# Turning probability tiles by a DMA round over DRAM and VectorE blocks instead of TensorE

## The chip, the cores and the metric

The kernel runs on one core of a Trainium2 chip. The metric is the device time in microseconds of one execution. The core has five engines with queues of their own, worked off in order: TensorE (PE; its weight loads are PEld), VectorE (DVE), ScalarE (ACT), GpSimd (POOL) and SyncE (SP, which here only issues DMAs). All DMAs of this kernel go through SP's queue and run on the core's 16 DMA engines.

## The reference

Two stages in float32. First an attention for 8 batches x 8 heads, 576 tokens, 64 values a head, whose scores below the row's maximum minus `tau` are dropped:

```
scores = q @ k.T / 8;  keep scores >= rowmax(scores) - tau
attn = exp(kept - rowmax) / (sum + 1e-9);  x = attn @ v
```

Then, for each batch, a gated layer over the 576 x 512 matrix x of all heads: `h = gelu(x @ w_in)` is split into u and v, v is normalized over its 512 columns and mixed over the tokens by `w_sg` (576 x 576, plus a bias), and the output is `x + (u * mixed v) @ w_out`.

## The kernel before, in words

Two heads are handled together as a pair; there are 32 pairs (n = 0 to 31), four of each batch. The 576 tokens are 4 row tiles of 128 and a tail of 64. A pair has 9 tiles (h, i): four whole row tiles of each head, and one (i = NM = 4) that holds the tails of both heads. For each tile:

- TensorE computes the scores of 128 rows against 576 keys into PSUM (L835; L810 and L824 in the first four pairs). From pair 4 on q and k are split into a high and a low fp32r part, which needs three products.
- VectorE takes the negated row maximum (L844), GpSimd makes the threshold of it (L850), ScalarE the exponentials (L871), written to a tile p in SBUF that holds 576 columns of each head, and VectorE zeroes what lies below the threshold and sums the rows (`select`, L878). There are two p tiles, used in turn.
- For the product with v the keys must lie on the partitions, so p is transposed. For each tile four 128x128 blocks go through TensorE into one PSUM bank (`transposes`) and ScalarE copies the bank to SBUF as the turned tile pt (`place`, L1001). The keys beyond 512 are turned and copied apart (`tail_transposes`, L1016).

In 27 pairs (n = 4 to 30; `by_rows` is true there, and `moved` with it) the whole row tiles of head 1 don't go to TensorE straight from p: `move` (L887) first copies their 512 columns by a DMA from SBUF to SBUF into a tile m of type fp32r, and TensorE turns m (L541, `turn_moved`). There are two rooms for m, used in turn. Tiles of head 0 and the tail tiles are turned as float32 (L538, `turn`).

P x V (`values`, L1027) then runs for 256 and for 320 columns of rows, both heads in two halves of the same bank. The row sums are inverted, sent to DRAM (L947) and fetched back spread over the partitions (L952 to L954); VectorE multiplies them in (L1036); the result x is kept as a high and a low part (L1047, L1052).

The gated layer of a batch (products at L1126) runs when the four pairs of its batch are done, in pieces between the scores of the next batch's pairs. The last batch's layer stands alone at the end.

All work is cut into steps, collected in `plan`. A table of 5476 places (`PLACES`) says in which order the steps are issued; each engine works off its own instructions in that order. Besides this, a planner in the kernel's build goes through the steps in that order with assumed durations and picks for each PSUM tile one of the 8 banks (`bank_of`).

Of the kernel before, what the change touches and what calls it, by code (L numbers as in the profile page):

```python
# [22 lines left out]
P = 128  # L23
# [11 lines left out]
PLACES = (  # L35
    "c-qZa3v^ZGmA>D9&b{ZJ`@YG2<^7NlNFWd1fdGO6Di&)Mb+lAkbzC#*npxAaUB#tst=h*b>ddqbOO{%7Xlt!)t!<}8+X@A-JmewBoA3q`z+iY9"
    "k~81_Pog|RAP^jna?id0+5f-y{`R*YCmzS~c-;Rx|H;k0cYf>q>TymHX#Yf@y-V5lQ+Ay4`N<y7NqbIRJxSO(d8w;yZSvDOb=${}Pdnwzr(Hkr"
    "oT|y`g|j_foZa5t?laH!^zdx-^4XqK?RF1z;G8aY#{O;=&h9{mp3}(Jjh=27y4BNmN(%JE{B!x^oZ*jidOGy79;XvG=ThkLoK4U9;^tg151dOI"
    "pC0++oR2@wNy5&>;&y5M=|w$V1n{&1;`AU-oll(yXX^2s<JgnCsB@NuGqSM@+`6LIxfS;yf1Dop(_=kd^36GCU+4xm=REm#0bxI@9?z$qKWE10"
    "Q>+KhS!jGlh@Fe$!8y$LT!cSe^=;>T)1@c=c+P@bw~6cYoClth>ZsFQy7YwC=fKVBQG7fX;?D()g*}=>x}V>ii>{;2X>;$HRr36QJKbRBUi&?#"  # L40
    "_ss6Eb3H#z!0ATBxxiDLi!tx4BA3*0ryIw6$5p4Ni=V3F=MT!IK=Cu`xaR_~Isc>E|Nk6!dg@2-z|g&h&t#5YiuixFbKG-*aqI=hdlHs&g4jFm"
    "IK7cmM!Tb4yD?!Oi<!z%cjIf<1&#(ni9VZ$s<Fzkec);W2mYbWOu=U#n_^7A_1fQmTV<jj-f0{d@_tS~3X~ywXmXpm3(0*+Zz?loYspZU@#c6="
    "!?aP;zJl2|KAJ!ArrKEYo7bSYZtB~0bp{YnkquA%=5YgA$VTGM2cNwoo`}FM#gfUp`-4|9g8Os(HI$k_Fp;{ad}O?Y+maYFX?R-{@FNPtGwwik"
    "IRyf@#~K0=e0ank2Q05DTmxSasV4ga8z$nhjj-VlBl}&OdMhJu!W%8ZAuJ8SXO6<c0yKgW3I9d}QH(bH7KobJ8Q_48GI@ks3bsFYgjNMhtaqrd"
    "IJgnVxNPRcRs%+v8MNNxG6vx9{OpU}sRcX&gR!gv%{0mM;R9F^1ta{E5Hc!}!fnq7fgJu<_T$3L(L)rs(%1~sAH%`$hkO>SP|K*>NEz7br@u&U"
    "rzLTozsly9zSxk9BL*#wU^hRLF!1XdlmiOp+CrjANz~T(9v8bqM$UR3S!{lQCcz|(1N=;Sfx~>L^05wf$jZ&e^9C$jjyG?>Vhf6R?xAcEPncz)"
# [12 lines left out]
    "K>f6Bj}92yy4ouegLK_dsE*p0CDrU!{PZsRA#m5@FG{Ddft8TzI9Rp98~JY09O}ufx&K+>c4Z^KTRA#U4N@jxycZ`HA@PEWi>dYm{3pEiq2D2N"
    "IE2!ef%$g4xugI)Yw$Bau|!{ciDLW<a18sDl&h@VR(pK<xp7rIyC(YGS;TEH)6#48!5UL)MSsF2#OQEP;Yzd^Y=FovzzS~4LNy!YD=^zr<!G$J"  # L60
    "JXozhvl@%oqKIl5>y0c*4+*xQ(p)f%bIZ0w;kW;j{!H8>S(q?a>oQYGxJctHe`3@tx++wwMzvoEaf@^v){Viw&CDMa=9!Ik_?8c*rLOi7KRZ|$"
    "-HRhia6`U<{_52)<Y3a=e?G8cD)rPc%_C+av{|Cgx^qzaCae-RYFQadA|8|JAlKzPCb6OG?#X^ytDBUUC19!e6Dr=z9N;M#<hA2AJbc9sgrGR@"
    "=?7SM?)ekH`-b8z4O0O_vP%|*VWIFHWyXGnjhm}UCFS^yDlYy=@o@6s4*W$2u?kBJ@-B<vU2RBykF__I)nMks!nfSoRgynb#iUT4kV=S;_jQ8e"
    "YV~J*#9;bmFmU$mn5CzTn@FjZibmgzmq-%wEvN=zo-lAMq1deo#NJ`YnU*UakRi3A_@V!1|C#i@w8S$1aw&N<s72~d7AJ!SJuvh`&{)H7u?ct?"
    "e(tV8%wp8z!2;|U$NW*D5c}L)f?Gc2-TF3=Ghqc5<ui{kEpNtiu0Mn+OLr0z{pgp_OI?n|U=?7%4vT|9vj$696b*F)`M6Yh{Y<r`eFa?GixHR)"
    "<)cl<Da%3~&H?M&jnixXixX5Zu<Cm9dVnE%3e_f^mILWV3%n=1QAU)hQCz6@U>ggccRJb3`1qs{%@v6+W6nhUjcX(tIZsH(GUrxme@3MCG9$K^"
    "3vMIxANis5(`K4!XV4%Bv#RXK+e$in>&<zZ2j#kab0MkuX0vG~@Umk55;x5^*0)M5=Y-34cbH(LC{QRd%AWmFP)2~k@77B_&~3ViF3VMmZA$7("
    "s8rXTC{f<V?!{D!&_VhW8O;3R;3#wX)~o0v!d`N5iPX6ab7}>W(rEg$BtyfVt|~Fx%&%l_f0cS({+eWat{$UulO|8w&o&*Hh>f~^mopqIq`p;Z"
    "Y!ny1fZ6gTiKe^s#MqHP25%AeP<biIv5wd(_~c7N>lfCqDBd}Y7FV#$7(N3>rM`KYeKIdda>y-%u}Zh=JUxuC0c7Fp^5v_T`F;GELzS5;z$!x5"
    "hDSIiYgBZ?%k{dRf&%(`iUsSdQY-?tz{&MAXQo_}wI&SRLZf&<3tCaRWlML+5;w~Ae%j#WAi(*`X74lQ!B0iX<g~B3<<;WQ{l}7S5SF=9B<Wd="  # L70
# [12 lines left out]
)
LAST_SCALE, SIGMA, SPREAD = 0.55, 1.155, 0.7
# [5 lines left out]
ROOMS = 2  # L90

# [5 lines left out]

ENGINES = ("tensor", "vector", "scalar", "gpsimd", "sync")

DELAY = dict(  # L100
    tensor=dict(tensor=0, vector=196, scalar=197, gpsimd=224, sync=190),
    vector=dict(tensor=230, vector=127, scalar=128, gpsimd=155, sync=120),
    scalar=dict(tensor=260, vector=146, scalar=153, gpsimd=170, sync=135),
    gpsimd=dict(tensor=205, vector=68, scalar=68, gpsimd=100, sync=67),
    sync=dict(tensor=1180, vector=907, scalar=978, gpsimd=983, sync=900),
)
BEGIN = 575.0
DMA_ISSUE, DMA_ISSUE_PART, DMA_START, DMA_LANES, DMA_BYTES = 525, 690, 650, 8, 250.0

WINDOW, WINDOW_BUSY, CLOCK, STREAM, PER_MATMUL = 10240 / 3, 3200 * P, 2.4, 2.333, 9.7  # L110

RESHAPE = 165


def time_of(engine, op, out, args, sums=False):

    n = out.size // out.shape[0]
    pointers = sum(a.size == a.shape[0] for a in args) if n > 1 else 0
    args = args or [out]
    half = out.shape[0] < P and n < 512  # L120
    if op == "memset":
        return n / 1.2 + (175 if engine == "gpsimd" and half else 35)
    if engine == "tensor":
        if op == "transpose":
            return n * (1 if args[0].dtype == F32R else 2) / CLOCK + (8 if args[0].dtype == F32R else 2.3)
        if args[0].dtype == F32:
            return n * 4 / CLOCK * (0.5 if min(out.shape[0], args[0].shape[0]) < P else 1.0) + 4
        return n / STREAM + PER_MATMUL
    if engine == "scalar":
        return n / 1.2 + (51 if args[0].psum else 93) + 93 * pointers + 115 * half  # L130
    if engine == "vector":
# [3 lines left out]
        elif op == "bn_stats":  # L135
            n = args[0].size // args[0].shape[0]
# [1279 lines left out]
```

## Time and profile before

| | |
|---|---|
| median of 3 runs | 961.41 us (961.38 to 962.68) |
| span of the profiled execution | 959.4 us |
| instructions | 20206 |
| DMA share of the 16 engines, dynamic queue | 45.6% |
| moved by DMA | 128.74 MB, mean 134 GB/s |
| HBM read, written | 46.40 MB, 9.56 MB |

The span runs from the first to the last instruction of the profiled execution; the time of that execution itself isn't recorded apart, and the median of the runs lies 2.0 us above its span. Busy time of an engine is the union of its instructions' durations. Matmuls overlap, so the mean duration of one is longer than its step in the chain. The clock of TensorE is granted in full (1.00) from 24 us on.

### The profile page before, as it was taken

The page shows a single profiled execution, that of the slowest core. Times are in us where ns is not written, and L with a number is a line of the kernel's source. Part 1 is how long each engine was busy: PE and PEld are TensorE (multiplying, and loading weights), DVE is VectorE, ACT ScalarE, POOL GpSimd, SP SyncE. Part 2 cuts the span into 40 slices and gives each one's busy share as a digit, 9 for nine tenths or more (in the row PEclk, how much of TensorE's full clock was granted, in tenths as well). Part 3 has the DMA queues.
Part 4 walks back from the last instruction along what each step waited for, and adds up shares of the span by engine and source line. Part 5 has one row for each costly group of instructions (what it writes and reads, how often), then busy time and mean ns, then how long its engine had stood idle before and what let it go on. Part 6 is the DMA issues. An engine that isn't in the chain of part 4 may idle for free.

```text
span 959.4 us, 20206 instructions
## 1 busy us (share of the span) xinstructions
PE 936.8 (98%) x6822; PEld 800.2 (83%) x6822; DVE 663.8 (69%) x1407; ACT 667.1 (70%) x1395; POOL 564.4 (59%) x997
## 2 busy tenths in 40 slices
PE   7999999999999999999999999999999999999998
PEld 4555889987798888998888898888889888898898
DVE  7899975767777567666786568766677757765451
ACT  5987886767875677665777677766787567764552
POOL 5865665555644577446763557536675366644467
PEclk9999999999999999999999999999999999999999
DMA  8353145465545553555445554456535455341001
GB/s 299 111 143 99 61 123 148 149 185 158 149 129 151 158 147 118 136 162 167 136 133 158 153 153 141 133 142 185 156 119 153 141 160 155 98 127 52 20 7 50
DMA packets 75791, 128.74 MB, mean 134 GB/s; under 512 B 16948, under 2 KB 25383, under 8 KB 75688
## 3 DMA queue, kind: packets, MB, share of 16 engines
q1 hardware_dynamic: 75688, 127.45, 45.6%
q8 instruction: 54, 0.88, 0.4%
q14 instruction: 49, 0.40, 0.1%
HBM read 46.40 MB, written 9.56 MB: 58 GB/s over the span
## 4 chain that ended last, share of the span: by engine, by line
PE 77%; ACT 7%; DVE 7%; DMA 3%; POOL 3%; issue 2%; SPq 0%; POOLq 0%; DVEq 0%; ACTq 0%
PE all_banks L1126 36%; PE all_banks L1027 14%; PE all_banks L835 14%; PE all_banks L538 8%; PE all_banks L541 3%; ACT p L871 2%; DVE nm L844 2%; DVE p L878 1%; DMA m<-p 1%; ACT pt L1001 1%; POOL ot L1331 1%; DMA qz<-qhi 1%; PE all_banks L810 1%; DVE gt L1112 1%; ACT vv L1218 1%
## 5 line engine op out<-in xcount | busy, mean ns | idle before, releaser
L871 ACT ACTIVATE p<-all_banks,nm 128x576 f32<-128x576 f32 x256 | 184.6, 742 | 92.5 <-DVE nm L844 90.6
L844 DVE TENSOR_REDUCE nm<-all_banks 128x1 f32<-128x576 f32 x288 | 208.7, 751 | 52.5 <-PE all_banks L835 43.3
L878 DVE SCALAR_TENSOR_TENSOR p<-all_banks,nm,p 128x576 f32<-128x576 f32 x256 | 204.2, 813 | 48.3 <-POOL nm L850 27.2
L1001 ACT ACTIVATE pt<-all_banks 128x512 f32<-128x512 f32 (+1 forms) x320 | 163.9, 554 | 19.4 <-PE all_banks L538 11.4
L835 PE MATMUL all_banks<-ks,qst 128*128 128x288 f32 x560 | 157.1, 314 | 1.4 <-ACT pt L1001 0.6
L850 POOL TENSOR_TENSOR nm<-columns,nm 128x1 f32<-128x1 f32 x288 | 55.0, 195 | 147.6 <-DVE nm L844 134.5
L1027 PE MATMUL all_banks<-pt,rv 128*64 128x256 f32 (+1 forms) x1024 | 137.8, 411 | 0.0
L835 PE MATMUL all_banks<-kl,qz 128*128 128x288 f32 x448 | 123.6, 295 | 0.0
L538 PE MATMUL all_banks<-ident_r,p 128*128 128x128 f32 x720 | 115.7, 276 | 3.1 <-DVE p L878 2.3
L835 PEld LDWEIGHTS all_banks<-ks,qst 128*128 128x128 f32 x560 | 102.1, 188 | 14.6 <-issue 6.9
L1126 PE MATMUL all_banks<-wsh,z 128*128 128x288 f32 (+2 forms) x512 | 113.4, 298 | 0.3 <-DVE uu L1109 0.3
L1027 PEld LDWEIGHTS all_banks<-pt,rv 128*64 128x64 f32 x1024 | 69.5, 136 | 48.6 <-issue 6.1
L538 PEld LDWEIGHTS all_banks<-ident_r,p 128*128 128x128 f32 x720 | 84.9, 141 | 20.0 <-issue 6.5
L1126 PEld LDWEIGHTS all_banks<-wsh,z 128*128 128x128 f32 x512 | 85.1, 188 | 2.4 <-issue 1.4
L835 PEld LDWEIGHTS all_banks<-kl,qz 128*128 128x128 f32 x448 | 84.5, 189 | 0.2
L1126 PE MATMUL all_banks<-xh,wih 128*128 128x288 f32 (+2 forms) x256 | 77.0, 301 | 0.2 <-ACT ot L1328 0.2
L1126 PE MATMUL all_banks<-gh,woh 128*128 128x288 f32 (+2 forms) x256 | 76.6, 300 | 0.0
L1126 PE MATMUL all_banks<-xl,wih 128*128 128x288 f32 (+2 forms) x256 | 76.0, 297 | 0.0
L1126 PE MATMUL all_banks<-xh,wil 128*128 128x288 f32 (+2 forms) x256 | 75.8, 296 | 0.0
L1126 PE MATMUL all_banks<-gh,wol 128*128 128x288 f32 (+2 forms) x256 | 75.8, 297 | 0.0
L1126 PE MATMUL all_banks<-wsl,z 128*128 128x288 f32 (+2 forms) x256 | 75.7, 297 | 0.0
L1126 PE MATMUL all_banks<-gl,woh 128*128 128x288 f32 (+1 forms) x240 | 70.7, 296 | 0.0
(147 smaller groups left out, 2202.2 us busy)
## 6 DMA issues: line engine op xcount, KB each, us to landing
m<-p SPq DMA_DIRECT2D x108, 256.0 KB
rk<-in_kT SPq DMA_DIRECT2D x32, 320.0 KB
rv<-in_vP SPq DMA_DIRECT2D x32, 320.0 KB
ks<-khi SPq DMA_DIRECT2D x56, 160.0 KB
rq<-in_qT SPq DMA_DIRECT2D x31, 288.0 KB
qz<-qhi SPq DMA_DIRECT2D x56, 144.0 KB
qst<-qhi SPq DMA_DIRECT2D x56, 144.0 KB
qst<-rq SPq DMA_DIRECT2D x56, 144.0 KB
```

The lines of the kernel that those rows point to most:

```text
L538: nc.tensor.transpose(out, x, ident_r.bitcast(F32))
L541: nc.tensor.transpose(out.bitcast(F32R), x, ident_r)
L810: nc.tensor.matmul(st["s", h, i][:, a, 0:HALF], st["q"][rows, qo:qo + P], st["k"][rows, lo:lo + HALF], start=True, stop=True)
L835: nc.tensor.matmul(sc[:, a, 0:HALF], w, x, start=(j == 0), stop=(j == len(terms) - 1))
L844: nc.vector.tensor_reduce(nmax, st["s", h, i][:, :, 0:HALF], AX.XY, ALU.max, negate=True)
L850: nc.gpsimd.tensor_tensor(thr, toff, st["nm", h, i], ALU.subtract)
L871: nc.scalar.activation(target(h, i), st["s", h, i][:, :, 0:HALF], AF.Exp, bias=st["nm", h, i])
L878: nc.vector.scalar_tensor_tensor(dst, st["s", h, i][:, :, 0:HALF], st["thr", h, i], dst, ALU.is_ge, ALU.mult, accum_out=st["l"][:, c:c + 1])
L1001: nc.scalar.activation(dst, src, AF.Copy)
L1027: nc.tensor.matmul(acc[h * D:(h + 1) * D, 0:w], st["v"][:, o:o + D], unit(h, a)[:, kt, 0:w] if kt < NM else tail_unit(a)[:, 0:w], start=(k ...
L1112: put("stt1", end, lambda: nc.vector.scalar_tensor_tensor(t["tmp"], t["tmp"], GELU_C, t["acc"], ALU.add, ALU.mult))
L1126: nc.tensor.matmul(st["acc"], *term(j), start=(j == 0), stop=(j == n - 1))
```

## The change

In the 27 pairs the whole row tiles of both heads are turned without TensorE. The constant `TURNED = (0, 1)` names the heads; `Q = 32` is the block's edge.

- `put_blocks` copies the 512 columns of a tile by one DMA into a DRAM tile d of the shape (4, 128, 128): column group, row, column. Each row of p goes out in four pieces of 512 bytes. There are four d tiles, used in turn.
- `get_blocks` reads d back by one DMA into a tile m (still two rooms): partition 32 g + j gets the rows 4 j to 4 j + 3 of column group g, 2 KB in one piece.
- `turn_blocks` is one VectorE transpose of 128x512 in 32x32 blocks, from m to the turned tile pt. Within a block it reads columns that lie four floats apart, and writes rows that lie four floats apart.

After this, partition p of block k of the turned tile holds key 4 p + k, where before it held key 128 k + p. So `layout` sends v's rows of those pairs in that order, and the tail tile of these pairs, which TensorE still turns, is read with a step of four columns. For the turned tiles no PSUM bank is filled and `place` is not called.

The order of issue is another one (5584 steps, table `ORDER`), and the PSUM banks come from a table too (`FIRST_BANKS`); the planner is gone from the build. In the new order a pair's last turns and its product with v stand among the scores of the next pair, and between the put and the get of a tile stand other DMAs of the same queue.

```diff
+TURNED = (0, 1)
+Q = 32
...
-        moved = by_rows
+        turned = TURNED if by_rows else ()
...
-        def move(h, i):
+        def put_blocks(h, i):
+
+            def f():
+                st["d", h, i] = dram.tile([P // Q, P, P], F32, tag="d", name=f"d{n}_{h}_{i}", bufs=4)
+                nc.sync.dma_start(st["d", h, i].rearrange("g q c -> q g c"),
+                                  st["p", i][:, h * KW:h * KW + MAIN].rearrange("p (g c) -> p g c", g=P // Q))
+            return f
+
+        def get_blocks(h, i):
             tag = slot("m", ROOMS)
 
             def f():
-                st["m", h, i] = ppool.tile([P, MAIN], F32R, tag=tag, name=f"m{n}_{h}_{i}")
-                nc.sync.dma_start(st["m", h, i].bitcast(F32), st["p", i][:, h * KW:h * KW + MAIN])
+                st["m", h, i] = ppool.tile([P, MAIN], F32, tag=tag, name=f"m{n}_{h}_{i}")
+                nc.sync.dma_start(st["m", h, i], st["d", h, i].rearrange("g (j a) c -> (g j) (a c)", a=P // Q))
+            return f
+
+        def turn_blocks(h, i):
+
+            def f():
+                a, j = divmod(i, 2)
+                nc.vector.transpose(unit(h, a)[:, :, j * P:(j + 1) * P].rearrange("p c (j a) -> p a c j", j=Q),
+                                    st["m", h, i].rearrange("p (a k c) -> p a c k", a=P // Q, k=Q))
             return f
...
-                    if moved and i < NM and h:
-                        turn_moved(out, st["m", h, i][:, kt * P:(kt + 1) * P])
-                    else:
-                        turn(out, pt[:, o + kt * P:o + (kt + 1) * P])
+                    x = pt[:, o:o + MAIN]
+                    turn(out, x.rearrange("p (k c) -> p c k", c=NM)[:, kt] if turned else x[:, kt * P:(kt + 1) * P])
...
-            if moved and i < NM and h:
-                at("move", g, move(h, i))
-            at("t", g, transposes(h, i))
-            at("hi", g, place(h, i))
+            if i < NM and h in turned:
+                at("move", g, put_blocks(h, i))
+                at("fetch", g, get_blocks(h, i))
+                at("turn32", g, turn_blocks(h, i))
+            else:
+                at("t", g, transposes(h, i))
+                at("hi", g, place(h, i))
...
+    strided = vv[:, :, :, :main].reshape(b, h // 2, 2, P, main // P, d).transpose(0, 1, 3, 4, 2, 5)
+    for n in range(WHOLE_SCORES, b * h // 2 - 1):
+        vm[divmod(n, h // 2)] = strided[divmod(n, h // 2)]
```

## Rows read from the trace of the kernel before

**Rows 1.** The page, busy us of each engine, share of the span, instructions.
```profile
PE 936.8 (98%) x6822; PEld 800.2 (83%) x6822; DVE 663.8 (69%) x1407; ACT 667.1 (70%) x1395; POOL 564.4 (59%) x997
```
**Rows 2.** Windows: stretch, length, busy PE, PEld, DVE, ACT, POOL, clock, DMA share, GB/s.
```profile
105.00:865.00 760.00, 751.90 (x5613) 659.68 (x5611) 530.90 (x1114) 538.51 (x1117) 444.69 (x781) 1.00 0.51 145
...
40.00:80.00 40.00, 37.25 (x235) 22.31 (x233) 38.69 (x87) 34.64 (x78) 27.38 (x51) 1.00 0.43 122
80.00:120.00 40.00, 39.02 (x258) 29.14 (x255) 37.91 (x87) 33.00 (x73) 22.69 (x53) 1.00 0.26 79
```
**Rows 3.** The chain of waits from 105 to 865 us, shares by line.
```profile
by line: PE all_banks L1126 40.6%; PE all_banks L835 16.6%; PE all_banks L1027 16.2%; PE all_banks L538 9.1%; PE all_banks L541 3.9%; DMA m<-p 1.7%; ACT pt L1001 1.1%; DMA qz<-qhi 1.1%; issue 1.0%; ACT p L871 1.0%; DVE nm L844 0.9%; DVE gt 
```
**Rows 4.** Pieces of the chain: start us, us, what.
```profile
504.00 0.30 PE all_banks L541 x4
...
527.24 0.44 PE all_banks L538 x4
```
**Rows 5.** Timeline of weight loads: start us, us, line, operation.
```profile
526.94 0.49 PEld L538 LDWEIGHTS all_banks<-ident_r,p 128*128 128x128 f32 x4
527.40 0.42 PEld L541 LDWEIGHTS all_banks<-ident_r,m 128*128 128x128 f32 x4
527.77 0.19 PEld L1126 LDWEIGHTS all_banks<-wsl,z 128*128 128x128 f32 x1
```
**Rows 6.** Groups by line from 105 to 865 us: busy us, mean ns, idle before.
```profile
L1001 ACT ACTIVATE pt<-all_banks 128x512 f32<-128x512 f32 x216 | 123.5, 594 | 14.4 <-PE all_banks L538 7.0 <-PE all_banks L541 6.6
```
**Rows 7.** Waits over the span: who for whom, us in total, times, longest.
```profile
ACT p L871 <- DVE nm L844: 90.6, 104, 3.2
DVE nm L844 <- PE all_banks L835: 43.3, 57, 4.7
```
**Rows 8.** Groups by line and form on VectorE, whole span.
```profile
L844 DVE TENSOR_REDUCE nm<-all_banks 128x1 f32<-128x576 f32 x288 | 208.7, 751 | 52.5 <-PE all_banks L835 43.3 <-ACT tt L1016 2.9 <-PE all_banks L810 1.4
...
L1199 DVE BATCH_NORM_STATS2 bn<-vv 128x6 f32<-128x512 f32 x32 | 22.1, 690 | 0.9
L1109 DVE SCALAR_TENSOR_TENSOR vv<-gt,all_banks 128x512 f32<-128x512 f32 x32 | 21.9, 683 | 11.0 <-ACT gt L1114 10.2 <-POOL z L1234 0.5
...
L1036 DVE TENSOR_TENSOR ir<-all_banks,ir 128x320 f32<-128x320 f32 x32 | 15.6, 486 | 5.6 <-PE all_banks L1027 4.7 <-DMA ir<-ld 0.7
L1036 DVE TENSOR_TENSOR ir<-all_banks,ir 128x256 f32<-128x256 f32 x32 | 13.3, 416 | 10.9 <-PE all_banks L1027 4.9 <-DMA out_T<-ot 4.5 <-DMA ir<-ld 1.3
...
L606 DVE TENSOR_SCALAR w<-room 128x512 uint32<-128x512 uint32 x8 | 5.8, 733 | 0.2
...
L598 DVE TENSOR_SCALAR all_banks<-room 128x512 uint32<-128x512 uint32 x8 | 5.5, 684 | 0.1
```
**Rows 9.** Timeline of VectorE, three reductions in a row.
```profile
533.59 2.10 DVE L844 TENSOR_REDUCE nm<-all_banks 128x1 f32<-128x576 f32 x3
```
**Rows 10.** DMA issues: out<-in, engine, count, KB each.
```profile
m<-p SPq DMA_DIRECT2D x108, 256.0 KB
```
**Rows 11.** Windows of the first loads, columns as in rows 2.
```profile
2.00:6.00 4.00, 3.18 (x8) 2.10 (x7) 1.75 (x5) 0.66 (x2) 0.69 (x2) 1.00 0.90 267
6.00:10.00 4.00, 2.49 (x9) 1.19 (x10) 3.45 (x11) 1.25 (x3) 2.40 (x3) 0.78 1.02 399
```
**Rows 12.** SP's issue times of single lines: ns min/median/max, first and last start.
```profile
L1334 SPq DMA_DIRECT2D out_T<-ot x64: 332/398/1101, 153.5 to 956.7; - x64
...
L730 SPq DMA_DIRECT2D rv<-in_vP x32: 328/432/768, 7.4 to 868.8; - x32
```
**Rows 13.** Waits of SP's queue, over the span.
```profile
SPq L887 <- DVE p L878: 143.3, 72, 17.0
SPq L1334 <- POOL ot L1331: 74.5, 18, 29.9
```
**Rows 14.** Timeline of SP's issues: row sums to DRAM, then back.
```profile
543.23 0.30 SPq L947 DMA_DIRECT2D ld<-ir  x1
546.00 0.47 SPq L952 DMA_DIRECT2D ir<-ld  x1
```

More of the change, by code (lines that the diff above doesn't have):

```diff
@@ L3 @@
 from collections import namedtuple
-from contextlib import ExitStack, contextmanager
+from contextlib import ExitStack
 from functools import partial
@@ new lines @@
+FIRST_BANKS = (
+    "c-k$JNdmwi2m=8D|NrA=VlQ13vOz>t_iXgk=`FpRk2qP8+ci;}t)h&*dhOjhvDK&4rkZnC$C0%iqrwNJPF=a}>{SQY>Qv!YhK_YW0Ti#h%nO6y>ST|P("
+    "_LjP`inF?QUrL#d25HZxvD?y??gtZKxQOFM@P^Bc3c6hO9eRfM5oYHJ*dW4mnl?sxxSB9uxMG61WlU);z!!Sg231MY7`Bu$%7;*)P-2)kfC6u3*TvPhe"
+    "XAnMLft)vJQr_nuV3AB1ls?-EchPe1b$;t)pxG-@#@}vWgIR0SpEvlbJ77R4FTD$mg*J$h)2<4@AexhY-`xf8Ki?3ofh}9HM(^od@uyUU+miav}{5&=)"
+    "VAH#%kxy$mmVp-Fi=4!M!L>g2ASg)-q%dWPxhtu-?`3!M<v8{S&^KlNd<DD^t4WuRJbk5~EDli>jyQNnVG6Pv70V=$K`Wp6Iz?mEm}={?oh=0px(gn2&"
+    "A847F"
@@ L107 @@
[L107 to L131, printed above, removed]
-        fast = op == "tensor_scalar" and not args[0].psum
-        if op == "tensor_reduce":
-            n = args[0].size // args[0].shape[0]
-        elif op == "bn_stats":
-            n = args[0].size // args[0].shape[0]
-        return n / (1.92 if fast else 0.96) + 69 + (60 if pointers else 0) + (60 if sums else 0)
-    if engine == "gpsimd":
-        if n == 1 and op == "tensor_tensor":
-            return 464 if pointers else 150
-        if len(out.shape) == 4:
-            return 149 + n + 140
-        return 149 + n * (1.0 if op == "tensor_scalar" else 2.103) + (115 if half or 1 < n < 8 else 0)
-    if out.tile.dram:
-        return out.size * 0.44
-    return out.size * (4 if n >= P else 8) / DMA_BYTES
@@ L149 @@
-class View:
-    def __init__(self, tile_, places, dtype):
-        self.tile, self.places, self.dtype = tile_, places, dtype
-        self.shape, self.size, self.psum = places.shape, places.size, tile_.psum
-    def __getitem__(self, key):
-        return View(self.tile, self.places[key], self.dtype)
-    def bitcast(self, dtype):
-        return View(self.tile, self.places, dtype)
-    def broadcast_to(self, shape):
-        return View(self.tile, np.broadcast_to(self.places, shape), self.dtype)
-    def rearrange(self, pattern, **sizes):
-        left, right = ([g.strip("()").split() for g in _groups(side)] for side in pattern.split("->"))
-        for group, total in zip(left, self.shape):
-            known = 1
-            for name in group:
-                known *= sizes.get(name, 1)
-            for name in group:
-                sizes.setdefault(name, total // known)
-        names = [name for group in left for name in group]
-        x = self.places.reshape([sizes[name] for name in names])
-        x = x.transpose([names.index(name) for group in right for name in group])
-        return View(self.tile, x.reshape([int(np.prod([sizes[n] for n in g])) for g in right]), self.dtype)
-    def area(self):
-        w = self.tile.width
-        first = self.places if self.tile.dram else self.places[0]
-        bits = np.zeros(w, np.uint8)
-        bits[first.ravel() % w] = 1
-        lo, hi = (int(self.places.flat[i]) // w for i in (0, -1))
-        return min(lo, hi), max(lo, hi) + 1, int.from_bytes(np.packbits(bits).tobytes(), "big")
@@ L487, in bank @@
         k = bank_of(name)
-        return psum.tile([P, 512], F32, tag=k, name=name) if k == BANKED else all_banks[:, k[0], :]
+        return psum.tile([P, 512], F32, tag=k, name=name) if k == BANKED else all_banks[:, k, :]
     def two_banks(name):
         k = bank_of(name)
-        return psum.tile([P, 2, 512], F32, tag=k, name=name) if k == BANKED else all_banks[:, k[0]:k[0] + 2, :]
+        return psum.tile([P, 2, 512], F32, tag=k, name=name) if k == BANKED else all_banks[:, k:k + 2, :]
     ident_r = cpool.tile([P, P], F32R, name="ident_r")
@@ L538, in turn @@
         nc.tensor.transpose(out, x, ident_r.bitcast(F32))
-    def turn_moved(out, x):
-        nc.tensor.transpose(out.bitcast(F32R), x, ident_r)
     def warm_up():
@@ L983, in f @@
                     out = tp[:, kt * P:(kt + 1) * P]
-                    if moved and i < NM and h:
-                        turn_moved(out, st["m", h, i][:, kt * P:(kt + 1) * P])
-                    else:
-                        turn(out, pt[:, o + kt * P:o + (kt + 1) * P])
+                    x = pt[:, o:o + MAIN]
+                    turn(out, x.rearrange("p (k c) -> p c k", c=NM)[:, kt] if turned else x[:, kt * P:(kt + 1) * P])
             return f
@@ L1360, in tile_threshold_attention_gated_mlp, with table @@
     issue(plan)
+def table():
+    data = np.frombuffer(zlib.decompress(base64.b85decode(ORDER)), np.uint8).astype(np.uint16).reshape(2, -1)
+    order = np.cumsum((data[0] * 256 + data[1]).astype(np.int16).astype(int)).tolist()
+    banks = list(zlib.decompress(base64.b85decode(FIRST_BANKS)))
+    assert sorted(order) == list(range(len(order)))
+    return order, banks
 _INS = ["qT", "kT", "vP", "w_in", "g_ln", "w_sgT", "b_sg", "w_out"]
@@ L1402 @@
     args.append(nc.dram_tensor("out_T", (b, h * d, s), F32, kind="ExternalOutput").ap())
-    planner = Planner()
-    tile_threshold_attention_gated_mlp(planner, *args, planner.rehearse, lambda name: BANKED)
-    order = planner.order()
+    order, banks = table()
+    banks = iter(banks)
     def issue(plan):
@@ L1412 @@
     with tile.TileContext(nc) as tc:
-        tile_threshold_attention_gated_mlp(tc, *args, issue, planner.bank_of.get)
+        tile_threshold_attention_gated_mlp(tc, *args, issue, lambda name: next(banks))
     r = run_bass_kernel_spmd(nc, [arrays], core_ids=[0])
```

338 lines of the change are left out of this document (82 added, 256 removed).

## The prediction

> **What bounds the kernel now.** I read the page's busy lines first, then the windows, then the chain of waits over the stretch that the change touches. The busy lines show TensorE at 98% of the span and every other engine at 70% or less [rows 1]. The windows say where: from 105 us, just before the first moved tile, to 865 us, just after the last, TensorE works 751.9 of 760 us at full clock, VectorE 530.9, ScalarE 538.5, and the DMA engines are busy half of the time [rows 2]. The chain over this stretch is made of TensorE pieces: the two transposing lines hold 9.1% (L538) and 3.9% (L541) of it, while no line of another engine has 2% [rows 3]. So here TensorE is the bound, and an instruction taken from it is worth its full time until something else is late. The change lies wholly in this stretch (27 pairs; pairs 0 to 3, pair 31, the weights and the last batch's end keep their work), so I leave the other 199.4 us of the span (959.4) as they are. The median of the runs, 961.4, is 2.0 us over the span; I add that at the end.
>
> **What it removes.** 27 pairs x 4 row tiles x 2 heads = 216 groups of four transposes: 108 of head 1 (L541, from the moved tile) and 108 of head 0 (L538, straight from p). On the chain four of L541 stand for 0.30 us and four of L538 for 0.44 us [rows 4]; by the starts of the weight loads, which hold the hand-over too, the four take 0.37 and 0.46 us [rows 5]. So 108 x (0.30 + 0.44) = 80 us, at most 108 x (0.37 + 0.46) = 90 us. I take 80: TensorE's work in the stretch falls from 751.9 to 672 us. ScalarE loses the 216 evacuations of 128x512 that follow, 123.5 us [rows 6], and falls to 415 us; I cost that gain at nothing, for ScalarE isn't the bound and its largest wait is for VectorE's maxima [rows 7]. The stride-4 reading of the tail tile's transposes, the other order of v's rows (made on the host) and the PSUM banks from a table instead of the planner I cost at nothing: they keep instruction counts. Bounds on each: the 27 x 4 tail transposes could at worst double, 27 x 0.44 = 12 us; below nothing there is no reason for either side.
>
> **What it adds on VectorE.** 216 transposes of 128x512 f32 from SBUF to SBUF, in 32x32 blocks. No row of before shows one. The nearest is the statistics over 128x512 f32 read from SBUF, 690 ns; a 512-element form that also reads PSUM takes 683 ns [rows 8]. Queued back to back an instruction costs some 0.05 us less than its mean (three reductions in 2.10 us against 751 ns each [rows 8, 9]), so the low end is 0.64 us. The high end is a pass at half rate: the 256- and 320-column products take 416 and 486 ns [rows 8], 1.09 ns a column, so 512 columns more would make 690 into 1250 ns. I take 0.69, the row that it is nearest to: 216 x 0.69 = 149 us, and VectorE's work in the stretch becomes 530.9 + 149 = 680 us, above TensorE's 672. The bound changes hands.
> How densely can VectorE run with this kernel's dependences? In the first turns of the program, where it sets the pace, it is busy 38.69 and 37.91 of 40 us [rows 2], that is 0.967 and 0.948. I take the lower, since the stretch adds waits for transfers: 680 / 0.948 = 717 us instead of 760, a gain of 43.
> [...]
>
> **What it adds in transfers.** One move of 256 KB inside SBUF for head 1 goes (108 of them [rows 10]), two for each of 216 tiles come: a put into DRAM in 512-byte pieces and a get of 2 KB rows. That is 432 x 262,144 B - 108 x 262,144 B = 84.9 MB more. The stretch moves 145 GB/s at a share of 0.51 [rows 2], 284 GB/s at full share; a burst of loads shows 399 GB/s at full share [rows 11]. So 213 to 299 us on top of 0.51 x 760 = 388: 601 to 687 us of 717. I take it as hidden, but only just; at the poor end it passes VectorE.
> On the SP queue 324 more issues come at about 0.4 us (0.398 for a store to DRAM, 0.432 for a load [rows 12]): some 130 us. SP has them to spare: it waits 143.3 us for p at the moves alone, 74.5 at one kind of store [rows 13].
> A get has to wait on SP until its put has landed. The like of it is there now: the row sums go to DRAM at 543.23 and are fetched at 546.00, 2.8 us later [rows 14]. Behind a waiting get stand the next puts, q's and k's copies, loads and stores of the same queue; who waits for them is ScalarE with the next p tile (two p buffers, free when both puts landed) and TensorE with the next pair's scores. A tile's way from p to its turned form is so about 2.8 + 2.8 + 0.7 us against one move before, and there are two rooms for moved tiles: eight turns of a pair over two rooms in 717 / 27 = 26.6 us leave 6.6 us for each, and a get and turn need about 2.8 + 0.7 + a place in VectorE's queue of 0.7. It fits, with 2.4 us to spare, so I add nothing; the new issue order puts P x V of a pair into the next pair's scores, where TensorE has other work.
>
> **Sum.** 959.4 - 760 + 717 + 2.0 = 918.6 us.
>
> **Rivals.**
> *TensorE stays the bound.* If a turn in the queue costs 0.6 us or less and VectorE waits for nothing, the whole 80 to 90 us come: 871 to 881, say 876. For it: ScalarE and the PSUM banks are relieved, and reductions wait 43.3 us for TensorE's scores now [rows 7]. Against it: it asks VectorE for 530.9 + 130 of 672 us, 98%, which no window shows.
> *The turn is slow (the other side).* It reads every fourth float of a row and writes every fourth float: 16 bytes a step on both sides. At the half rate of 1.25 us VectorE gets 530.9 + 270 = 801, over 0.948 = 845 us: 1046 us in all. It decides from (760 x 0.948 - 530.9) / 216 = 0.88 us a turn: above that the kernel is slower than now. Against it: the one strided form here, the weight words written at a step of 8 bytes, takes 733 ns for 512 elements, near the 684 of its dense neighbour [rows 8]; nothing shows 16 bytes.
> [...]
> *The transfers become the bound.* At the poor end they are 687 us of work, and where a get waits for its put the engines stand empty; at 0.90 busy, which the loads' first window shows [rows 11], the stretch takes 763 us and the kernel 964. For it: 512-byte pieces on one side, one in-order queue. Against it: full share does occur.
>
> **How the numbers follow.** Forecast 0.52, with its own range 893 (0.64 us a turn, 0.967 dense: 530.9 + 138 = 669, over 0.967 = 692) to 945 (0.69 us at 0.914 dense); TensorE bound 0.08; transfers 0.21, spread over 945 to 1000; slow turn 0.19, mostly beyond 1000. The range 880 to 1005 leaves out most of the last and a part of the second, about 0.2. A change of 0.2% (2 us) is about what the measurement tells from none. Faster: 0.50 + 0.08 + 0.02 = 0.60; same 0.05, where the forecast and the transfers' case meet; slower 0.16 + 0.19 = 0.35.
>
> **What would show it.** Right: VectorE busy 93% or more of the turned stretch and TensorE down to about 0.94 of it, the turn at 0.64 to 0.72 us, the chain with VectorE's lines at tens of per cent, transposes x468 instead of x1332, ScalarE near 543 us. Wrong: a turn above 0.88 us; a DMA share over 0.9 with VectorE idle and waiting for the moved tile; TensorE still at 98%; or VectorE waiting for SP's late gets while neither engine nor DMA is full.

## The result and the profile after

The changed kernel takes 969.18 us (median of 4, 965.4 to 971.18) against 962.04 us (961.38 to 963.25) for the kernel before in the same comparison: a ratio of 1.0069, with a 95% interval of 1.0046 to 1.0092. It is slower by 0.7%, where 918.6 us, a faster kernel, was forecast. Times here and below are medians of the executions at a granted TensorE clock of 0.96 or more; the one execution below it (0.655, 1192.11 us, of the kernel with the whole computation) is left out of its median.

The page of the changed kernel, engine by engine (us, share of the span, instructions; the span is 969.4 us), and its one DMA queue (packets, MB, share):
```profile
PE 889.2 (92%) x5958; PEld 728.3 (75%) x5958; DVE 856.8 (88%) x1623; ACT 560.1 (58%) x1179; POOL 563.9 (58%) x997
...
q1 hardware_dynamic: 205288, 212.40, 76.0%
```
Against [rows 1] TensorE has 864 transposes less and lost its 98%. VectorE rose from 663.8 to 856.8 us, ScalarE fell by 107 us.

The window of the turned stretch, columns as in [rows 2]:
```profile
105.00:865.00 760.00, 693.74 (x4659) 576.83 (x4658) 709.99 (x1303) 426.01 (x884) 436.70 (x771) 0.99 0.88 252
```
VectorE is now the fullest engine, 710 of 760 us (0.934), TensorE has 66 us without work instead of 8, and the DMA engines went from a share of 0.51 to 0.88.

The groups of the changed kernel (xcount, busy us, mean ns, idle before), first the turn, then the maxima that stood first in [rows 8]:
```profile
L625 DVE STREAM_TRANSPOSE pt<-m 128x512 f32<-128x512 f32 x216 | 244.5, 1141 | 10.6 <-DMA m<-d 10.1
L567 DVE TENSOR_REDUCE nm<-all_banks 128x1 f32<-128x576 f32 x288 | 207.5, 746 | 20.8 <-PE all_banks L558 14.5
```
One turn takes 1141 ns, where 690 was assumed. It hardly ever waits for its data (10.1 us in all), and the maxima wait for TensorE 14.5 us instead of 43.3 [rows 7]: VectorE has its work ready and is behind with it. The waits of the others say the same (who for whom, us, times, longest; ScalarE's was 90.6 us before [rows 7], GpSimd's 134.5):
```profile
POOL nm L573 <- DVE nm L567: 179.3, 130, 5.0
ACT p L594 <- DVE nm L567: 142.3, 106, 4.2
...
PE all_banks L764 <- DVE pt L625: 10.5, 18, 1.5
```
The followed chain of the changed kernel breaks off early (TensorE's pieces in it are 7% of the span, and there is little else), so no share is read from it.

How densely turns stand, from VectorE's timeline in the changed kernel (start us, us):
```profile
711.17 0.76 DVE L567 TENSOR_REDUCE nm<-all_banks 128x1 f32<-128x576 f32 x1
711.84 1.12 DVE L625 STREAM_TRANSPOSE pt<-m 128x512 f32<-128x512 f32 x1
712.83 0.80 DVE L601 SCALAR_TENSOR_TENSOR pm<-all_banks,nm,pm 128x576 f32<-128x576 f32 x1
```
The reduction's record ends at 711.93, after the turn began at 711.84; the turn's ends at 712.96, after the next began at 712.83. Records of VectorE overlap by about a tenth of a us where work is queued. So the whole span's busy time grew by 856.8 - 663.8 = 193.0 us while the turns alone are busy for 244.5: **net, a turn costs 193.0 / 216 = 0.89 us**. This is the figure that belongs in the forecast's sum, where a turn is added to VectorE's busy time, and it falls on the break-even that the forecast gave for it (0.88).

First and last start of the put and of the turn (ns min/median/max, then us):
```profile
L609 SPq DMA_DIRECT2D d<-p x216: 359/426/1586, 96.5 to 870.5; - x108
L625 DVE STREAM_TRANSPOSE pt<-m x216: 1055/1143/1232, 104.6 to 885.4; 128x512 f32<-128x512 f32 x108
```
Before, this work ran from 106.1 (first move) to 859.8 us (last transpose of m), 753.7 us; now it runs from 96.5 (first put) to 885.4 (last turn), 788.9 us. That is 35.2 us more. It begins 9.6 us earlier, and behind it 84.0 us follow instead of 99.6. 35.2 - 9.6 - 15.6 = 10.0 us, the difference of the two spans.

### The profile page after: what moved, and what is told of

It is laid out like the page before. It is cut to its first block, busy times and chain, and to the rows that moved or that the text cites. A ratio compares the mean times of both kernels' runs of the same rounds, so it can differ in the third digit from the quotient of the medians.

```text
span 969.4 us, 18918 instructions
## 1 busy us (share of the span) xinstructions
PE 889.2 (92%) x5958; PEld 728.3 (75%) x5958; DVE 856.8 (88%) x1623; ACT 560.1 (58%) x1179; POOL 563.9 (58%) x997
## 5 line engine op out<-in xcount | busy, mean ns | idle before, releaser
L594 ACT ACTIVATE p<-all_banks,nm 128x576 f32<-128x576 f32 x256 | 186.4, 740 | 160.6 <-DVE nm L567 142.3
L625 DVE STREAM_TRANSPOSE pt<-m 128x512 f32<-128x512 f32 x216 | 244.5, 1141 | 10.6 <-DMA m<-d 10.1
L567 DVE TENSOR_REDUCE nm<-all_banks 128x1 f32<-128x576 f32 x288 | 207.5, 746 | 20.8 <-PE all_banks L558 14.5
L558 PE MATMUL all_banks<-ks,qst 128*128 128x288 f32 x560 | 161.5, 320 | 23.9 <-DVE p L601 9.5
L764 PE MATMUL all_banks<-pt,rv 128*64 128x320 f32 (+1 forms) x1024 | 139.8, 412 | 12.7 <-DVE pt L625 10.5
L866 PE MATMUL all_banks<-wih,xh 128*128 128x512 f32 x160 | 65.3, 410 | 2.7 <-DVE pm L601 2.1
L264 PE MATMUL all_banks<-ident_r,p 128*128 128x128 f32 x288 | 57.7, 284 | 10.2 <-DVE p L601 7.4
```

What stands on the lines that cost most here:

```text
L264: nc.tensor.transpose(out, x, ident_r.bitcast(F32))
L558: nc.tensor.matmul(sc[:, a, 0:HALF], w, x, start=(j == 0), stop=(j == len(terms) - 1))
L567: nc.vector.tensor_reduce(nmax, st["s", h, i][:, :, 0:HALF], AX.XY, ALU.max, negate=True)
L594: nc.scalar.activation(target(h, i), st["s", h, i][:, :, 0:HALF], AF.Exp, bias=st["nm", h, i])
L625: nc.vector.transpose(unit(h, a)[:, :, j * P:(j + 1) * P].rearrange("p c (j a) -> p a c j", j=Q), st["m", h, i].rearrange("p (a k c) -> p ...
L764: nc.tensor.matmul(acc[h * D:(h + 1) * D, 0:w], st["v"][:, o:o + D], unit(h, a)[:, kt, 0:w] if kt < NM else tail_unit(a)[:, 0:w], start=(k ...
```

## The experiments

Each ratio is against the kernel before, with its 95% interval. Where no diff of the layout is shown, it is that of the kernel it builds on.

**The price of a turn: one side dense, then both.** The tile m is read, and pt written, at a step of four floats. The other order of v's rows (made on the host) lets the turn read with a step of one; another order of the query rows lets it write so. These three kernels leave out what that order asks of the rest: with the dense read the tail's keys don't match v's rows, and with the dense write the output's rows stand in another order. They show times, not a kernel to use; the one that computes everything comes further down.

Read side (v's rows follow on the host):
```
-  unit(...).rearrange("p c (j a) -> p a c j", j=Q),  m.rearrange("p (a k c) -> p a c k", ...)
+  unit(...).rearrange("p c (j a) -> p a c j", j=Q),  m.rearrange("p (a c k) -> p a c k", ...)
```


> The turn reads 32 neighbouring columns of m for a block instead of every fourth (v's rows follow; the tail tile of the turned pairs keeps the step of four, so its keys don't match). Theory 1 (VectorE sets the pace, because reading at a 16-byte step halves the turn's rate): the turn falls from 1141 ns to 640 to 700, VectorE's busy share of the turned stretch from 0.93 to below 0.90, the time to 900 to 935 us. Theory 1b (the writing side's step is the slow one): the turn stays at 1100 to 1150 ns and the time at 965 to 971. Theory 2 (the transfers set the pace, busy 0.88 of the stretch): the turn may fall, the time stays at 960 to 971 and VectorE waits for m.

Write side:
```
-  unit(...).rearrange("p c (j a) -> p a c j", j=Q)
+  unit(...).rearrange("p c (a j) -> p a c j", j=Q)
```


> The turn writes the 32 rows of a block side by side instead of four floats apart (the output's rows stand in another order within a tile). Theory 1 (reading step): the turn stays at 1100 to 1150 ns, the time at 965 to 971. Theory 1b (writing step): the turn falls to 640 to 700 ns, the time to 900 to 935. Theory 2 (transfers): the time stays at 960 to 971 whatever the turn does.

Both:

> Both sides of the turn dense (tail keys and row order as in the two kernels before it). Theory 1 and 1b: the turn at 600 to 700 ns, the time 900 to 935 us. If either side alone is enough to halve the rate, only this kernel is faster. If the 32x32 transpose of floats runs at half rate whatever the steps are: 1141 ns and 965 to 971 us here too. Theory 2: 960 to 971.

Measured: 962.65 us, ratio 1.0007 (0.999 to 1.0023), with the dense read; 970.3 us, 1.009 (1.0073 to 1.0106), with the dense write; 942.32 us, 0.9791 (0.9762 to 0.9819), with both. From the pages, the engines and the turn with the dense read:
```profile
PE 890.4 (92%) x5958; PEld 732.2 (76%) x5958; DVE 840.0 (87%) x1623; ACT 561.0 (58%) x1179; POOL 562.8 (58%) x997
...
L625 DVE STREAM_TRANSPOSE pt<-m 128x512 f32<-128x512 f32 x216 | 236.7, 1108 | 16.1 <-DMA m<-d 15.7
```
the turn with the dense write:
```profile
L625 DVE STREAM_TRANSPOSE pt<-m 128x512 f32<-128x512 f32 x216 | 237.3, 1103 | 10.3 <-DMA m<-d 9.8
```
the engines and the turn with both:
```profile
PE 880.0 (93%) x5958; PEld 726.7 (77%) x5958; DVE 778.4 (83%) x1623; ACT 560.7 (60%) x1179; POOL 561.3 (60%) x997
...
L625 DVE STREAM_TRANSPOSE pt<-m 128x512 f32<-128x512 f32 x216 | 150.6, 701 | 34.0 <-DMA m<-d 33.0
```
and the window of the stretch with both:
```profile
105.00:865.00 760.00, 710.23 (x4864) 598.62 (x4862) 651.12 (x1339) 438.80 (x915) 449.50 (x795) 0.99 0.90 257
```
A 16-byte step on either side alone makes the turn 1.10 us, on both 1.14, on none 0.70. So the step is the cause of the slow turn, and one slow side is enough. The rate isn't halved: a turn with one slow side takes 1.6 times the dense one. As the third expectation has it for this case, only the kernel with both sides dense is faster than the kernel before, but its 942.3 us lie outside the 900 to 935 given.

The two slow sides aren't alike in what the next instruction feels. A turn and the instruction behind it, with the dense read, with the dense write and with both (start us, us):
```profile
704.81 1.09 DVE L625 STREAM_TRANSPOSE pt<-m 128x512 f32<-128x512 f32 x1
705.74 0.75 DVE L601 SCALAR_TENSOR_TENSOR pm<-all_banks,nm,pm 128x576 f32<-128x576 f32 x1
```
```profile
712.45 1.08 DVE L625 STREAM_TRANSPOSE pt<-m 128x512 f32<-128x512 f32 x1
713.46 0.78 DVE L601 SCALAR_TENSOR_TENSOR pm<-all_banks,nm,pm 128x576 f32<-128x576 f32 x1
```
```profile
300.63 0.70 DVE L625 STREAM_TRANSPOSE pt<-m 128x512 f32<-128x512 f32 x1
301.26 0.72 DVE L567 TENSOR_REDUCE nm<-all_banks 128x1 f32<-128x576 f32 x1
```
The next instruction starts 0.93 us after the turn's start with the dense read, 1.01 us with the dense write, though the records are nearly alike, and 0.63 us with both. This fits the times: the dense read gains 6 to 7 us on the changed kernel, the dense write nothing.

The dense, the dense-read and the changed kernel also give the slope. Net, by the busy sums (778.4, 840.0 and 856.8 less 663.8, over 216), a turn costs 0.53, 0.82 and 0.89 us, and the times are 942.3, 962.65 and 969.2 us. So 61.6 us of VectorE's work cost 20.3 us, and 16.8 more cost 6.5: **a third to four tenths of VectorE's work shows in the time**, not all of it. With the dense turn VectorE is busy only 651 of 760 us and waits for m 33 us: something else is late as well. TensorE is the fullest engine there again, with 710 of 760 us (0.934); it was at 0.989 before, so that it sets the pace isn't shown.

**Are the transfers the other thing?** The put in pieces of 2 KB instead of 512 bytes, with the dense turn and with the strided one:
```
-  dma_start(d.rearrange("g q c -> q g c"), p[...].rearrange("p (g c) -> p g c", g=P // Q))
+  dma_start(d.rearrange("g (j a) c -> (g j) (a c)", a=P // Q), p[...])
```


> As e3_dense_both, but the put writes each row in one piece of 2 KB instead of four of 512 bytes (same bytes; the blocks' grid is not turned, so the values are wrong). Theory B (with a dense turn the transfers set the pace): the 512-byte packets go, the DMA share of the stretch falls from 0.90 to about 0.85 or less, the time from 942 to 925 or less. Theory A alone (VectorE sets the pace in e3 too) or C (the order on SP's queue): the time stays at 936 to 944.

> The changed kernel with its strided turn, the put in pieces of 2 KB (values wrong as in e5_wide_put). Theory A (VectorE sets the pace of the changed kernel): the DMA share falls, the time stays within 962 to 971 us. Theory B (transfers already set the pace there): 955 or less.

Measured: 938.09 us, 0.9763 (0.9745 to 0.978), and 968.25 us, 1.0072 (1.005 to 1.0094). The stretch with the dense turn:
```profile
105.00:865.00 760.00, 713.99 (x4910) 604.27 (x4911) 652.35 (x1344) 441.94 (x924) 452.74 (x800) 0.99 0.84 258
```
and with the strided one:
```profile
105.00:865.00 760.00, 695.66 (x4673) 578.91 (x4672) 710.73 (x1306) 426.84 (x885) 438.02 (x773) 0.99 0.83 252
```
The DMA share falls by 0.05 to 0.06. With the dense turn the ratio goes from 0.9791 to 0.9763, and the intervals overlap, so a gain isn't shown and the 925 us of theory B didn't come. The interval of the strided one is nearly that of the changed kernel (1.0046 to 1.0092). So a lower load on the DMA engines, at the same bytes, doesn't speed up the changed kernel.

**One move instead of put and get** (the get reads p inside SBUF):
```
-  dma_start(d, p...)          # put
-  dma_start(m, d...)          # get
+  dma_start(m, p[..., 512 columns])
```


> The put is left out and the get reads p inside SBUF (one move of 2 KB rows, no DRAM; the blocks' grid is not turned, so the values are wrong); the turn stays. Theory 1: VectorE still has its 1141 ns turns, the time stays within 962 to 971 us though the DMA share falls from 0.88 to about 0.65. Theory 2: the time falls by 25 us or more, to 945 or less.

Measured: 1050.73 us, 1.0926 (1.0877 to 1.0976). The DMA share falls to 0.55 and VectorE waits 0.4 us for m, and yet the kernel is slower, by a new wait:
```profile
ACT p L594 <- DMA m<-p: 150.8, 49, 7.5
```
Without the tiles in DRAM p isn't free until one of the two rooms for m is, and SyncE waits 187.0 us for VectorE's turns before it can issue a move. The four DRAM tiles are buffers. Neither theory's time came, and as a test of the transfers this is inconclusive.

**The puts from ScalarE's queue**, with the dense turn (`nc.sync` becomes `nc.scalar` in the put):

> As e3_dense_both, with the puts issued from ScalarE's queue instead of SP's. Theory C (a get that waits on SP for its room or its put holds back the next puts, and so the p tiles): the time falls from 942 to 930 or less. Theory B: no change of the bytes, 938 to 946. If ScalarE is held up by waiting for the selected p tile before it may issue: slower, 950 or more.

Measured: 1012.34 us, 1.054 (1.0516 to 1.0565). VectorE waits 41.5 us for m instead of 33.0, and a new wait stands on ScalarE, which now issues behind p:
```profile
ACT p L594 <- DMA d<-p: 28.7, 20, 2.9
```
The time is that of the expectation's last case, 950 or more. The put's way isn't relieved; what of the 70 us is this wait and what the order isn't told apart.

**Head 1 alone through DRAM**, head 0 on TensorE at the place of its get, the banks picked anew:
```
-TURNED = (0, 1)
+TURNED = (1,)
```


> Only head 1 is turned by the DMA round and VectorE (108 of 216 tiles, the strided turn); head 0 goes through TensorE and ScalarE as before, at the place in the order where its get stood, and the banks are given anew. Values are right. Theory A: VectorE's work in the stretch falls by 108 x 1.03 = 111 us and TensorE, with 108 x 0.44 = 48 us more than in the changed kernel and 32 to 40 less than before, is the bound again: 925 to 945 us. If the order of issue itself costs time: 950 or more.

Measured: 1099.96 us, 1.1425 (1.1375 to 1.1474). Here no engine is full (window of the stretch):
```profile
105.00:865.00 760.00, 678.74 (x4530) 565.78 (x4530) 559.22 (x1085) 429.45 (x898) 385.79 (x688) 0.97 0.58 159
```
The 925 to 945 us of theory A didn't come; the other case, 950 or more, did. ScalarE waits 93.7 us for TensorE's turned blocks, as the issue order was made for other work; that the order makes the whole loss isn't shown. On the price of the turn the run shows nothing.

**The whole computation with short steps.** Query columns laid out in turned order by the host, so that the turn writes densely; the put in pieces of 256 bytes, as two DMAs, so that it reads at 8 bytes; tail copies and row sums to match:
```
-  dma_start(d: "g q c -> q g c",  p: "p (g c) -> p g c")
+  for u in range(2):
+      dma_start(d: "g q (u x) -> q g u x"[:, :, u],  p: "p (u g x) -> p u g x"[:, u])
-  transpose(pt: "p c (j a) -> p a c j",      m: "p (a k c) -> p a c k")
+  transpose(pt: "p (u c) (a j) -> p a u c j", m: "p (a u k c) -> p a u c k")
```


> The changed kernel's whole computation, with the steps of the turn shortened on both sides: the host lays the query columns of the 27 pairs out in turned order, so that the turn writes its blocks side by side (4-byte step), and each put becomes two DMAs whose pieces are 256 bytes, so that the turn reads with an 8-byte step instead of 16; the tail's copies, the row sums (four reads of two copies of their rows instead of three) and the rows of v follow the new order. Theory A (the 16-byte step is what made the turn dear, and a step of 8 bytes is still cheap): a turn of 0.70 to 0.80 us, VectorE 650 to 675 of the 760 us, and 938 to 955 us, near the 942 of the kernel with both sides dense. Rival B (any step other than 4 bytes costs the half rate): turns of 1.10 us as with the one dense side, 960 to 975 us. Rival C (the 216 puts more on SyncE's queue, with pieces of half the size, make the transfers the bound): turns of 0.70 to 0.80 us but VectorE waiting for m for over 60 us (33 in the kernel with both sides dense), and 955 us or more.

Measured: 1010.19 us (median of five), 1.0514 (1.0488 to 1.0539). The turns were cheap (702 ns) and the time was not. So the kernel was profiled once more, and two kernels were run between it and the dense one:

> The kernel with the whole computation and the short steps of the turn once more, for a profile at the usual clock: its only profile so far has TensorE's granted clock at 0.65 all over, so its waits are those of a slow TensorE. Its turns took 702 ns there, so theory A's price of a turn holds and its time (1011 against 938 to 955) does not. If the transfers hold it up (rival C), VectorE waits for m for over 60 us and fewer than 640 of the 760 us are busy on it; if the wait is elsewhere (the row sums with a fourth read, the tail's copies), VectorE waits little for m and TensorE or ScalarE waits for rows of r or for the tail's tiles.

> The kernel with both sides of the turn dense (942 us; output in another order) with each put as two DMAs of half the bytes, in pieces of 512 bytes as before: 216 issues more on SyncE's queue, nothing else. If the number of issues is what made the kernel with the whole computation slow, 990 us or more; if the queue has room for them, 940 to 950 us.

> The same two DMAs, but each in pieces of 256 bytes, as in the kernel with the whole computation (keys in another order within a tile, so the output's values are not the reference's): twice the pieces of the one before at the same bytes and issues. If the size of the pieces is what costs, this one is 40 us or more above the kernel with two puts of 512-byte pieces; if neither the issues nor the pieces cost anything, both stand at 940 to 950 us and the cost of the kernel with the whole computation lies in its row sums and tail copies.

Measured: 1010.97 us (two executions), 1.0507 (1.0469 to 1.0546); two puts in 512-byte pieces 979.62 us, 1.0196 (1.015 to 1.0242); two puts in 256-byte pieces 998.5 us, 1.0379 (1.0347 to 1.0412). The turn with two puts of 512-byte pieces:
```profile
L626 DVE STREAM_TRANSPOSE pt<-m 128x512 f32<-128x512 f32 x216 | 151.0, 703 | 64.7 <-DMA m<-d 63.9
```
the window of its stretch:
```profile
105.00:865.00 760.00, 686.03 (x4578) 572.79 (x4577) 627.44 (x1282) 418.04 (x870) 429.92 (x761) 0.98 0.88 249
```
and the turn of the whole computation:
```profile
L626 DVE STREAM_TRANSPOSE pt<-m 128x512 f32<-128x512 f32 x216 | 151.4, 704 | 86.3 <-DMA m<-d 85.8
```
An 8-byte step on the read side is as fast as a dense one (704 against 701 ns); on the write side it wasn't tried. The signs of rival C came true: VectorE waits for m over 60 us and is busy 602 of the 760. From the dense kernel's 942 us on, 216 issues more cost 37 us at the same bytes (between the two cases of that expectation), the smaller pieces 19 us more (half of the 40 expected), and all that the whole computation adds, the row sums and tail copies above all, the last 12. VectorE's wait for m goes with it: 33.0, 63.9, 81.5, 85.8 us.

SyncE's timeline with two puts shows what an issue is on that queue (start us, us):
```profile
402.27 1.16 SPq L1075 DMA_DIRECT2D out_T<-ot  x1
403.53 0.92 SPq L610 DMA_DIRECT2D d<-p  x2
404.54 0.44 SPq L619 DMA_DIRECT2D m<-d  x1
```
A put or a get takes 0.44 to 0.46 us of the queue here and the store 1.16, one after the other. Summed over the records of the stretch, SyncE issues for 356 us of the 760 in the kernel before, 497 in the changed one, 520 with the dense turn, 605 with two puts and 632 with the whole computation; its pauses over 0.3 us sum to 273, 173, 144, 65 and 38 us. In the last two kernels the queue has almost no slack left; how much later a put is issued for it wasn't measured.

**Taking issues off SyncE's queue.** The 64 stores of the output go to GpSimd's queue (`nc.sync` becomes `nc.gpsimd`), with the dense turn and in the changed kernel:

> The kernel with both sides of the turn dense (942 us, output in another order), with the 64 stores of the output issued from GpSimd's queue, behind GpSimd's own addition that makes them ready, instead of from SyncE's. In the dense kernel SyncE waits 58 us for those additions, with puts and gets queued behind, and 64 issues stand on it. If SyncE's queue is what keeps the dense kernel from the 919 us that the forecast gave for a turn of 0.69 us: by the 0.17 us that each further issue cost, 11 us less, and up to 20 us of the waits: 915 to 935 us, VectorE's wait for m below 33 us. If what is left there is the transfers' own time, or if an issue costs GpSimd enough to make thresholds late: 940 us or more.

> The changed kernel with its 16-byte steps, and the 64 stores of the output issued from GpSimd's queue instead of SyncE's. The theory that VectorE with turns of 1.14 us sets the pace: VectorE's share of the stretch stays near 0.93 and the time moves by 0 to 8 us, 960 to 970. If SyncE's queue sets it: the same gain as in the dense kernel or more, below 955 us, with VectorE's wait for m falling from 10 us to little.

Measured: 994.96 us, 1.0341 (1.0318 to 1.0364), and 1021.35 us, 1.0627 (1.0605 to 1.0649). Neither gained: both are some 52 us slower, the first as in its last case (940 or more), the second outside all that was expected. There was also less to gain than was thought: of the 58 us that SyncE waits for GpSimd's additions in the dense kernel, 5.1 lie in the stretch and 53.3 behind it, where no put or get follows. With the dense turn VectorE does wait less for m (23.4 us), but GpSimd has 64 stores to issue (ns min/median/max), and VectorE's waits for GpSimd's row sums and thresholds grow from 6.3 and 5.1 us. The stores on GpSimd's queue, then the waits, with the dense turn:
```profile
L1074 POOL DMA_DIRECT2D out_T<-ot x64: 543/598/789, 171.8 to 990.5; - x64
```
```profile
DVE ir L652 <- POOL l L646: 18.9, 10, 5.9
...
DVE p L601 <- POOL nm L573: 18.2, 16, 3.8
```
The rival of the first expectation (an issue makes GpSimd late) is seen in these waits; that they make the whole 52 us isn't shown. The test doesn't tell what SyncE's queue costs the dense kernel.

## Why the prediction was wrong, step by step

**TensorE was the bound before; its transposes go.** Right: 864 instructions went and the maxima wait for it less. TensorE's busy sum fell by 47.6 us (56.8 in the dense kernel), less than the 80 taken from the chain. Since another engine sets the pace, the 80 were not put to the test.

**ScalarE's gain costed at nothing.** Right: 107 us of its busy time went (123.5 forecast for the stretch), and it waits for VectorE's maxima 142.3 us instead of 90.6.

**"I take 0.69" for one turn: the step that failed first.** Its record shows 1.14 us; in the sum, where neighbours overlap, it counts 0.89. To the record the high end (1.25) was the nearer one, and the slow-turn rival had the cause, the 16-byte step (1103 to 1141 ns with it, 701 without). The forecast set the 16-byte step aside because an 8-byte step was cheap in [rows 8]; an 8-byte step is cheap here too (704 ns), and says nothing of 16. With 0.89 and nothing else changed the forecast's sum gives (530.9 + 193.0) / 0.948 = 763.6 us for the stretch and 965.0 us in all, against 969.2 measured. The slow-turn rival's 1046 was too high, since it took a turn at 1.25 us and added the whole of it to VectorE's time.

**"680 / 0.948 = 717", with all else hidden ("so I add nothing"): the step that the first one covered.** The dense kernel tests it. By the same sum a net turn of 0.53 us asks VectorE for (530.9 + 114.6) / 0.948 = 680.9 us and gives 882.3 us; measured 942.3, with VectorE at 0.857 of the stretch. On a straight line between the runs at 0.53 and 0.82 us, a turn of just 0.69 us would give an estimated 942.3 + 0.16 x 216 x 0.33 = 954 us. So, by this estimate, of the 50.6 us that the forecast missed about 15 are the turn's price and about 35 a bound that the sum didn't have. That the sum comes out at 965 with the right price is in part luck: two of its terms were off in opposite ways, for the turned work took 32 us longer than the sum has it, and 25 us less stood outside it.

**What the 35 us are.** The forecast gave put and get 2.8 us each to land, and SyncE some 130 us more of issues, which it had to spare. The issues were sized right (497 - 356 = 141 us), though of the 74.5 us that it counted at the stores only 8.3 lie in the stretch. The landing was sized too low. The chain of the dense kernel from 105 to 865 us, by line in shares of the 760 us, and pieces of it (start us, us); it can be followed back to 277 us only:
```profile
by line: PE all_banks L866 15.2%; PE all_banks L558 6.7%; PE all_banks L764 6.2%; DMA d<-p 5.6%; issue 4.3%; DMA m<-d 4.3%; DVE p L601 3.1%; DVE nm L567 3.0%; DVE pt L625 2.0%; ACT p L594 1.8%; DMA ks<-khi 1.7%; DMA qz<-qhi 1.6%; PE all_ban
...
310.94 4.78 DMA d<-p
319.88 4.95 DMA m<-d
...
605.30 5.46 DMA d<-p
636.29 3.10 DMA m<-d
```
Puts and gets hold 9.9% of the 760 us on it, in eighteen pieces of 2.7 to 5.5 us; TensorE's first three lines hold 28.1%. With the longest get, 4.95 us, a room needs 4.95 + 0.7 + 0.7 = 6.35 of its 6.6 us, and of the 2.4 us to spare 0.25 are left; with the mean of the eight gets, 4.1 us, 1.1. What SyncE's gets and puts wait for in the dense kernel (us, times, longest):
```profile
SPq L618 <- DMA d<-p: 51.6, 61, 2.6
SPq L609 <- DVE p L601: 33.3, 50, 3.2
...
SPq L618 <- DVE pt L625: 17.3, 35, 2.4
```
The gets wait most for their own puts to land, 51.6 us, and least of the three for a room to be turned, 17.3 us. Two runs show that this path is sensitive (37 us for 216 more issues, 19 for smaller pieces). Not shown is how the 35 us divide between landing, SyncE's queue, the two rooms and the new order of issue, which no run tested apart: the runs that moved work off the path each put a new wait on ScalarE or GpSimd. A third room was not tried.

**VectorE's density.** 0.948 was taken, 0.934 measured in the changed kernel: nearly right where VectorE sets the pace.

**Transfers "hidden, but only just".** Right for the changed kernel: a share of 0.88, VectorE waits for m 10.1 us, and wider puts change nothing (968.25 us against 969.18). The transfers' rival (964 us) is near in time only; it wanted VectorE idle and waiting for m.

**The 199.4 us outside left as they are.** Wrong by 25 us, in the kernel's favour: the work starts 9.6 us earlier, and behind the last turn 15.6 us less remain. The longer stretch took up other work: TensorE has 4868 instructions in it, where the 5568 of before less 864 would be 4704. It is why 35 us of longer stretch became 10 of span.

## What to carry to other kernels

Before work moves to an engine that doesn't have the operation yet, look at the byte step of both its sides: a cheap 8-byte step is no evidence for a 16-byte one, and one slow side is enough (here 704 ns with 8 bytes on the read side, 1103 and 1108 with 16 on one side, 701 dense). Price an instruction by what it adds to the engine's busy sum, not by its record, and say at which price the change breaks even; here the measured price, 0.89 us where the record has 1.14, stood on the forecast's point (0.88), and the kernel that broke even had 0.82. And when the bound is to change hands, look for the third resource just below it (here probably a put, a get and their place in one in-order queue): it decides what the fix of the first mistake is worth, 27 us here instead of the 83 of the forecast's sum.

## What the runs showed that was not expected

- A turn of 128x512 f32 takes 701 ns dense, 704 with an 8-byte step on the read side, 1103 and 1108 ns with a 16-byte step on one side, 1141 with it on both: in the record the second slow side is almost free. By what it adds to VectorE's busy sum a slow write side alone makes it 0.82 us, a slow read side alone 0.89, both 0.89.
- Dense, a turn takes 701 ns, 1.37 ns a column, and 0.63 us from its start to the next instruction's where one is queued behind it.
- VectorE's records overlap their neighbours' by about 0.1 us when work is queued, and 244.5 us of turns made 193.0 us of added busy time.
- 216 more DMA issues, at the same bytes in the same pieces, cost 37 us (0.17 us each) on SyncE's queue, whose 1164 issues in the stretch take 605 us.
- The puts and gets of 256 KB on the dense kernel's chain take 2.7 to 5.5 us each, where 2.8 was forecast; but the tiles in DRAM are buffers, and the kernel without them was 82 us slower than the changed one.
